# Ten output tiles in place of five, and another sequence of transfers on the sync engine's queue, in an RWKV-6 attention feeding a leaky-ReLU feed-forward layer

## The chip, the core and the metric

The kernel runs on one core of a Trainium2 chip. The core has a matrix engine (TensorE, PE in the profile, with its weight loads listed apart as PEld), three engines for elementwise work (VectorE or DVE, ScalarE or ACT, GpSimd or POOL), and a sync engine (SyncE or SP), whose only work here is to issue transfers. Sixteen DMA engines move the data between the chip's memory and the on-chip buffers. Each engine works through its own list of instructions in order, and semaphores tell one engine what another has finished. The metric is the device time of one execution in microseconds (us), as the median of several runs; less is better.

## What is computed

Four sequences of 768 positions with 8 heads of 48 numbers go through a recurrence with a state of 48x48 per head, and the result of every position, 384 numbers wide, goes through a feed-forward layer of width 2048.

```python
def _attn_ref(r, k, v, w, u):
    B, H, S, D = r.shape                      # 4, 8, 768, 48
    state = np.zeros((B, H, D, D))
    for t in range(S):
        kt, vt, rt, wt = ...
        cur = np.einsum('bhd,bhe->bhde', u[None] * kt, vt)
        y[:, :, t] = np.einsum('bhd,bhde->bhe', rt, state + cur)
        state = wt[:, :, :, None] * state + np.einsum('bhd,bhe->bhde', kt, vt)
    return y

def _moe_ref(x, w_in, w_out):                 # x: 3072 x 384
    h = x @ w_in                              # w_in: 384 x 2048
    g = np.maximum(0.01 * h, h)
    return g @ w_out                          # w_out: 2048 x 384
```

## The kernel before

**Tiling.** The 768 positions of each of the four sequences are cut into chunks of 128, which makes 24 chunks, numbered 0 to 23 in the order in which they are worked on (`seq`). Chunks 0 to 3 go two at a time through `pair`, the others through `single`. A chunk needs four loads, w, k, r and v (192 KB each, line 704 in `single`), which share one tile of the pool `in`. From them come the logarithm of the decay (ACT, line 714, tile `lw`), its running sum (PE, lines 720 and 723), its exponentials (ACT, lines 741, 746 and 750), the scaled r and k (DVE, line 403, tile `rk`), their transpose (tile `rkT`; for thirteen chunks a transposing DMA from SP, line 767, for the others PE and a copy, lines 414 to 421), the scores (PE, line 860), the masked scores (DVE, line 791, tile `m`), the bonus term of the current position (POOL, lines 433, 437 and 445, with a sum on DVE, line 441, tiles `ru`, `dg` and `vs`), the decayed state (POOL, line 778, tile `sb`), the new state (PE, line 801, and DVE, lines 814 and 816, tile `s`), and the attention's output (PE, lines 827 and 832, and DVE, line 478, tile `y`). That output is transposed into a tile of the pool `xT` (PE, ACT or DVE, lines 464 to 471; for six chunks a transposing DMA from SP, line 845).

**The layer behind it.** Fourteen blocks of one or two chunks follow (`blocks`). A block's first product reads its `xT` tile and the first weights (PE, line 1026); ACT applies the leaky ReLU (line 1041) into a tile of the pool `g`. The second product is plain for the first seven blocks (PE, line 1056; copied out on lines 1067 and 1069; stored on line 1073). For the last seven blocks `seven` does it with seven half-size products instead of eight (PE, line 956), with sums of `g` on DVE beforehand (line 937) and differences of the weights prepared once (line 906); the results are combined on ACT and DVE (lines 970, 972 and 977) in tiles of the pool `o` and stored on line 1009. Each chunk ends in a store of 192 KB from a tile of `o`; one of the last goes in two halves, so that there are 25 stores.

**What sets the order.** Nothing is reordered by a scheduler. Each piece of work is a step of a `Plan`; the table `ORDER` lists the 1124 steps by number, and `FORCE` names the engine where a step has a choice. `Plan.order` walks through `ORDER`, hands each step that opens a tile the tile of its pool that the planner thinks free first, and the steps are then written out in that order. So every engine's list is the part of `ORDER` that falls to it. The planner's times (`LOAD`, `STORE`, `TRK` and so on) choose only which tile of a pool is taken. Waits are put in by the framework: a transfer into a tile waits for the last reader of what was there, a store waits for the engine that filled the tile.

**SP's queue.** All transfers but one tiny one stand in one list on SP: 142 of them, which are loads, weights, transposes and stores. SP issues them strictly in that order. A transfer whose wait isn't over holds up all that stand behind it. It also waits, before each, for the transfer eight places earlier to have landed, as there are eight completion semaphores in turn.

```python
    make("s", 6, [128, NP, 2, D], F32)
    make("xT", 6, [128, KT, max(blocks) * L], BF16)
    make("o", 5, [128, DM], F32)
```

## Time and profile before

| | |
|---|---|
| median of 3 runs | 178.51 us (178.13 to 179.82) |
| the profiled execution: its own time | 179.84 us |
| the profiled execution: span from first to last instruction | 178.1 us |
| granted TensorE clock | 1.000 of full speed |
| bytes moved | 33.89 MB on SP's queue; 25.17 MB read, 4.72 MB written |

The profile is one execution. The profile's page gives each engine's busy time, then the span in forty slices with one digit of busy share for each, then the DMA queues, the chain of work that ended last, and the costliest groups of instructions. Beside the page the trace can be asked for the instructions of an engine in order of time, for busy times by stretch, and for who waited for whom. In the rows in order of time the columns are start and duration in us, engine, line, operation, tile written <- tiles read, shape, how many alike stand in the row, and in brackets the engine's idle time ahead of it and what ended that. SPq is SP's sequencer, whose rows last from the start of an issue until the next can go.

### The profile page before, as it was taken

The page shows a single profiled execution, that of the slowest core. Times are in us where ns is not written, and L with a number is a line of the kernel's source. Part 1 is how long each engine was busy: PE and PEld are TensorE (multiplying, and loading weights), DVE is VectorE, ACT ScalarE, POOL GpSimd, SP SyncE. Part 2 cuts the span into 40 slices and gives each one's busy share as a digit, 9 for nine tenths or more (in the row PEclk, how much of TensorE's full clock was granted, in tenths as well). Part 3 has the DMA queues.
Part 4 walks back from the last instruction along what each step waited for, and adds up shares of the span by engine and source line. Part 5 has one row for each costly group of instructions (what it writes and reads, how often), then busy time and mean ns, then how long its engine had stood idle before and what let it go on. Part 6 is the DMA issues. An engine that isn't in the chain of part 4 may idle for free. (4 is left out here: it accounts for less than half of the span.)

```text
span 178.1 us, 5529 instructions
## 1 busy us (share of the span) xinstructions
PE 169.0 (95%) x2155; PEld 139.5 (78%) x2158; DVE 142.6 (80%) x300; ACT 113.1 (64%) x262; POOL 106.1 (60%) x143
## 2 busy tenths in 40 slices
PE   6899999996999999999999999999999999999992
PEld 2555788754778877777779899799898888899992
DVE  7698735275699889879879999989999889966862
ACT  5787769814777793796369964676966671248500
POOL 5999846369759668869778384291572872700000
PEclk9999999999999999999999999999999999999999
DMA  5999998999999899899899999896999995533014
GB/s 139 261 272 342 350 298 167 358 227 211 195 190 201 154 191 229 149 199 199 169 212 171 204 192 278 161 205 136 201 205 176 204 156 109 177 90 103 32 37 145
DMA packets 115885, 34.25 MB, mean 192 GB/s; under 512 B 108305, under 2 KB 115090, under 8 KB 115858
## 3 DMA queue, kind: packets, MB, share of 16 engines
q1 hardware_dynamic: 115856, 33.89, 88.9%
q8 instruction: 17, 0.28, 0.7%
q14 instruction: 10, 0.08, 0.2%
q10 hardware_dynamic: 2, 0.00, 0.0%
HBM read 25.17 MB, written 4.72 MB: 168 GB/s over the span
## 5 line engine op out<-in xcount | busy, mean ns | idle before, releaser
L1026 PE MATMUL ps<-xT,w_in_b 128*128 128x256 bf16 (+1 forms) x672 | 71.3, 257 | 0.1
L1041 ACT ACTIVATE g<-ps 128x512 bf16<-128x512 f32 x96 | 54.5, 599 | 18.6 <-PE ps L1026 16.8
L1026 PEld LDWEIGHTS <-w_in_b 128*128 128x128 bf16 x672 | 56.8, 98 | 7.4 <-ACT w_in_b L340 0.6
L433 POOL TENSOR_TENSOR ru<-in,ub 128x384 f32<-128x384 f32 x24 | 23.9, 999 | 13.1 <-DVE dg L441 6.6
L1056 PE MATMUL ps<-w_out_b,g 128*128 128x384 bf16 x160 | 31.4, 326 | 0.0
L403 DVE TENSOR_TENSOR rk<-in,ps 128x384 bf16<-128x384 f32 x48 | 25.0, 548 | 6.0 <-ACT ps L750 2.2
L437 POOL TENSOR_TENSOR ru<-ru,in 128x384 f32<-128x384 f32 x24 | 23.8, 1000 | 5.0 <-DMA in<-in_r_dram 4.3
L791 DVE TENSOR_TENSOR m<-ps,maskb 128x512 bf16<-128x512 f32 x40 | 25.3, 683 | 0.6 <-PE ps L860 0.6
L445 POOL TENSOR_TENSOR vs<-in,dg 128x384 f32<-128x384 f32 x20 | 16.9, 844 | 11.3 <-DVE dg L441 5.1
L778 POOL TENSOR_TENSOR sb<-s,a 128x384 bf16<-128x384 f32 x18 | 14.8, 828 | 10.6 <-ACT g L1041 4.6
L1056 PEld LDWEIGHTS <-g 128*128 128x128 bf16 x160 | 14.1, 97 | 7.0 <-issue 0.2
L956 PEld LDWEIGHTS <-g 128*128 128x128 bf16 x224 | 18.4, 98 | 0.3
L441 DVE TENSOR_REDUCE dg<-ru 128x8 f32<-128x384 f32 x24 | 13.0, 547 | 5.0 <-POOL ru L437 4.8
L453 POOL CAST vb<-in 128x384 bf16<-128x384 f32 x24 | 13.2, 554 | 4.6 <-DMA in<-in_v_dram 4.0
L972 ACT COPY o<-ps 128x192 f32<-128x192 f32 x17 | 5.4, 317 | 16.0 <-PE ps L956 13.9
L714 ACT ACTIVATE lw<-in 128x384 bf16<-128x384 f32 x20 | 10.0, 520 | 7.0 <-DMA in<-in_w_dram 7.0
L977 DVE TENSOR_TENSOR o<-ps,o 128x192 f32<-128x192 f32 x35 | 11.6, 352 | 3.5 <-DMA out_dram<-o 1.3
L956 PEld LDWEIGHTS <-in 128*128 128x128 bf16 x168 | 13.6, 98 | 0.8 <-DVE in L937 0.5
L478 DVE TENSOR_TENSOR y<-ps,vs 128x384 bf16<-128x384 f32 x20 | 10.8, 552 | 2.2 <-PE ps L832 1.5
L750 ACT ACTIVATE ps<-ci 128x384 f32<-128x384 f32 x20 | 9.8, 491 | 3.8 <-DVE ci L732 3.1
L732 DVE TENSOR_TENSOR ci<-ps,lw 128x384 f32<-128x384 f32 x20 | 10.9, 551 | 1.0 <-PE ps L720 0.6
L956 PE MATMUL ps<-in,in 128*128 128x192 bf16 x112 | 11.4, 247 | 0.3 <-DVE in L937 0.3
(105 smaller groups left out, 255.2 us busy)
## 6 DMA issues: line engine op xcount, KB each, us to landing
out_dram<-o SPq DMA_DIRECT2D x23, 192.0 KB, 3.3
in<-in_w_dram SPq DMA_DIRECT2D x20, 192.0 KB, 4.7
in<-in_k_dram SPq DMA_DIRECT2D x20, 192.0 KB, 4.3
in<-in_r_dram SPq DMA_DIRECT2D x20, 192.0 KB, 4.6
in<-in_v_dram SPq DMA_DIRECT2D x20, 192.0 KB, 4.2
in<-in_moe_w_out_dram SPq DMA_DIRECT2D x4, 768.0 KB, 6.8
in<-in_moe_w_in_dram SPq DMA_DIRECT2D x2, 768.0 KB, 9.8
in<-in_moe_w_in_dram SPq DMA_DIRECT2D x4, 384.0 KB, 8.2
```

The lines of the kernel that those rows point to most:

```text
L403: (nc.gpsimd if e == "POOL" else nc.vector).tensor_tensor(out=o, in0=x, in1=i, op=ALU.mult)
L433: lambda e: nc.gpsimd.tensor_tensor(out=ru.t[:], in0=kv(), in1=ubv, op=ALU.mult),
L437: lambda e: nc.gpsimd.tensor_tensor(out=ru.t[:], in0=ru.t[:], in1=rv(), op=ALU.mult),
L441: lambda e: nc.vector.tensor_reduce(out=dg.t[:], in_=ru.t[:], axis=AX.X, op=ALU.add),
L445: lambda e: nc.gpsimd.tensor_tensor(out=vs.t[:], in0=vv(), in1=dg.t[:].unsqueeze(2).to_broadcast([128, H, D]), op=ALU.mult),
L453: {"POOL": 0.56}, lambda e: nc.gpsimd.tensor_copy(out=vb.t[:], in_=vv()),
L778: lambda e: nc.gpsimd.tensor_tensor(out=sb.t[:].rearrange("p g a d -> p (g a) d"), in0=s_in.t[:].rearrange("p g a d -> p (g a) d"), in1=a_ ...
L791: lambda e, par=par: nc.vector.tensor_tensor(out=m.t[:, par, :, :], in0=sc[par].t[:].rearrange("p (g t) -> p g t", g=NP), in1=maskb[:].uns ...
L956: nc.tensor.matmul(o(), lhsT=x()[:, i, :], rhs=y()[:, i, :], start=fresh, stop=(stop and i == ii[-1]), skip_group_check=True)
L1026: nc.tensor.matmul(hp.t[:, a * N : (a + 1) * N], lhsT=w_in_b[:, t, (j + a) * 128 : (j + a + 1) * 128], rhs=xb.t[:, t, 0:N], start=(a == 0 ...
L1041: lambda e, hp=hp, g=g, j=j, J=J, N=N: nc.scalar.activation(out=g.t[:, j : j + J, 0:N], in_=hp.t[:, 0 : J * N].rearrange("p (a n) -> p a n ...
L1056: nc.tensor.matmul(op.t[:, 0:DM], lhsT=g.t[:, j, off : off + 128], rhs=w_out_b[:, j, :], start=(j == 0), stop=(j == NJ - 1))
```

## The change

Three pools change their size: `o` from five tiles to ten, `xT` from six to three, `s` from six to five. In `ORDER`, the numbers of SP's steps are put into other places from about the 200th entry on. `FORCE`, the planner's times and all other code stay.

```diff
-    736, 770, 756, 139, 141, 140, 737, 176, 184, 186, 187, 148, 150, 164, 170, 171, 168, 169, 175, 185, 190, 191, 192,
+    736, 770, 756, 139, 141, 140, 737, 176, 148, 184, 186, 175, 187, 150, 164, 170, 171, 168, 169, 185, 190, 191, 192,
...
-    make("s", 6, [128, NP, 2, D], F32)
+    make("s", 5, [128, NP, 2, D], F32)
...
-    make("xT", 6, [128, KT, max(blocks) * L], BF16)
-    make("o", 5, [128, DM], F32)
+    make("xT", 3, [128, KT, max(blocks) * L], BF16)
+    make("o", 10, [128, DM], F32)
```

On PE, DVE, ACT and POOL the instructions stand in the same order as before; only the numbers of the tiles that they use differ in places. On SP the first 34 transfers are the same, and from the 35th on the sequence differs. Of the 25 stores, 13 stand among the first 124 transfers before and 9 in the changed kernel. The three places below are all on SP. A name such as `in8_82` is the ninth tile of the pool `in`, and the same chunk's loads can have another tile in the two kernels.

The first place is the 35th to the 45th transfer. Before, it reads as follows; `in7`, `in8`, `in10` and `in0` hold chunks 8, 9, 11 and 10, and `in2` and `in6` hold chunks 6 and 7.

```order
L1073 DMA out_0_dram<-o3_149 128x384
L704 DMA in2_76<-in_v_dram 128x8x48
L704 DMA in6_80<-in_v_dram 128x8x48
L704 DMA in7_81<-in_k_dram 128x8x48
L704 DMA in8_82<-in_w_dram 128x8x48
L704 DMA in10_84<-in_w_dram 128x8x48
L704 DMA in7_81<-in_r_dram 128x8x48
L704 DMA in8_82<-in_k_dram 128x8x48
L704 DMA in8_82<-in_r_dram 128x8x48
L704 DMA in7_81<-in_v_dram 128x8x48
L704 DMA in0_74<-in_w_dram 128x8x48
```

In the changed kernel the same stretch is this; here `in10` holds chunk 10 and `in0` chunk 11.

```order
L704 DMA in2_76<-in_v_dram 128x8x48
L704 DMA in8_82<-in_w_dram 128x8x48
L704 DMA in6_80<-in_v_dram 128x8x48
L704 DMA in7_81<-in_k_dram 128x8x48
L704 DMA in7_81<-in_r_dram 128x8x48
L704 DMA in8_82<-in_k_dram 128x8x48
L704 DMA in8_82<-in_r_dram 128x8x48
L704 DMA in10_84<-in_w_dram 128x8x48
L1073 DMA out_0_dram<-o2_144 128x384
L704 DMA in7_81<-in_v_dram 128x8x48
L704 DMA in0_74<-in_w_dram 128x8x48
```

The store has gone from the front, chunk 9's r is two places earlier (43rd to 41st), chunk 10's w three places earlier (45th to 42nd), and chunk 11's w five places later (40th to 45th).

The second place is around the transposes of chunks 16 and 17 (`rk2` and `rk1`), the 84th to the 93rd transfer before.

```order
L704 DMA in7_81<-in_v_dram 128x8x48
L704 DMA in0_74<-in_k_dram 128x8x48
L704 DMA in0_74<-in_w_dram 128x8x48
L1073 DMA out_0_dram<-o2_148 128x384
L704 DMA in10_84<-in_k_dram 128x8x48
L1073 DMA out_0_dram<-o1_147 128x384
L1073 DMA out_0_dram<-o3_149 128x384
L1073 DMA out_0_dram<-o0_146 128x384
L767 DMA_TRANSPOSE rkT1_98<-rk2_94 128x8x128
L767 DMA_TRANSPOSE rkT0_97<-rk1_93 128x8x128
```

In the changed kernel they are the 89th and the 90th transfer, and the rows from the 83rd are these.

```order
L704 DMA in7_81<-in_v_dram 128x8x48
L1073 DMA out_0_dram<-o9_151 128x384
L704 DMA in8_82<-in_k_dram 128x8x48
L704 DMA in0_74<-in_k_dram 128x8x48
L1073 DMA out_0_dram<-o6_148 128x384
L704 DMA in0_74<-in_w_dram 128x8x48
L767 DMA_TRANSPOSE rkT0_97<-rk2_94 128x8x128
L767 DMA_TRANSPOSE rkT1_98<-rk1_93 128x8x128
```

Two stores stand among the six transfers ahead of the two transposes where four stood among the eight, and none stands directly ahead.

The third place is the loads of chunks 20 to 23. Before, the 109th to the 119th transfer are these, with chunk 20 in `in6`, 21 in `in4`, 22 in `in2` and 23 in `in7`.

```order
L1009 DMA out_0_dram<-o4_150 128x384
L704 DMA in4_78<-in_k_dram 128x8x48
L704 DMA in7_81<-in_w_dram 128x8x48
L704 DMA in2_76<-in_k_dram 128x8x48
L704 DMA in4_78<-in_r_dram 128x8x48
L704 DMA in2_76<-in_w_dram 128x8x48
L704 DMA in2_76<-in_r_dram 128x8x48
L704 DMA in6_80<-in_v_dram 128x8x48
L767 DMA_TRANSPOSE rkT1_98<-rk1_93 128x8x128
L767 DMA_TRANSPOSE rkT0_97<-rk4_96 128x8x128
L704 DMA in4_78<-in_v_dram 128x8x48
```

In the changed kernel the same work is the 106th to the 115th, with chunk 20 in `in4`, 21 in `in6` and 22 in `in7`.

```order
L1073 DMA out_0_dram<-o0_142 128x384
L704 DMA in6_80<-in_k_dram 128x8x48
L704 DMA in4_78<-in_v_dram 128x8x48
L704 DMA in7_81<-in_w_dram 128x8x48
L704 DMA in6_80<-in_r_dram 128x8x48
L704 DMA in7_81<-in_k_dram 128x8x48
L767 DMA_TRANSPOSE rkT0_97<-rk1_93 128x8x128
L704 DMA in7_81<-in_r_dram 128x8x48
L767 DMA_TRANSPOSE rkT1_98<-rk4_96 128x8x128
L704 DMA in6_80<-in_v_dram 128x8x48
```

Chunk 22's w is five places earlier (114th to 109th) and chunk 21's v four (119th to 115th), with eight stores ahead of them in place of twelve; chunk 23's r, a little further on, goes from the 122nd place to the 118th. The stores that have left these stretches stand behind the last load, among the 125th to the 137th transfer.

78 rows, old and new, of the table ORDER are left out of this document.

## The prediction

> **What bounds the kernel now.** I read the page first, then busy times by stretch, then PE's instructions in order of time, then what stands before each of PE's stops.
>
> ```profile
> PE 169.0 (95%) x2155; PEld 139.5 (78%) x2158; DVE 142.6 (80%) x300; ACT 113.1 (64%) x262; POOL 106.1 (60%) x143
> ...
> DMA  5999998999999899899899999896999995533014
> ...
> q1 hardware_dynamic: 115856, 33.89, 88.9%
> ```
>
> ```profile
> 50.00:75.00 25.00, 24.74 (x319) 19.38 (x318) 23.10 (x44) 17.63 (x41) 18.29 (x22) 1.00 0.98 185
> ...
> 100.00:125.00 25.00, 24.72 (x334) 22.68 (x332) 23.24 (x47) 16.62 (x44) 11.97 (x15) 1.00 0.94 196
> 125.00:150.00 25.00, 24.27 (x324) 21.70 (x323) 23.80 (x48) 16.22 (x43) 15.48 (x19) 1.00 0.95 180
> 150.00:170.00 20.00, 20.00 (x231) 18.61 (x230) 15.56 (x37) 9.86 (x19) 3.90 (x5) 1.00 0.32 95
> ```
>
> PE (the third number of a stretch) is close to full from 50 us on. The 16 DMA engines are as full: their share, the last but one number, is 0.94 to 0.98 up to 150 us, and the page's digits are 8s and 9s till then. So there are two full resources, PE and the one queue that SP feeds. What the change can touch is the places where PE stops because that queue is late. These are PE's rows around its stops.
>
> ```profile
> 41.51 0.32 PE L720 MATMUL ps<-lw,trev 128*128 128x384 bf16 x1 [1.85 <-ACT lw L714]
> ...
> 67.02 0.83 PE L1026 MATMUL ps<-xT,w_in_b 128*128 128x256 bf16 x6
> 68.11 0.40 PE L860 MATMUL ps<-rkT 48*128 48x128 bf16 x8 [0.26 <-DVE rkT L419]
> ...
> 113.89 0.40 PE L860 MATMUL ps<-rkT 48*128 48x128 bf16 x8
> 114.56 0.40 PE L860 MATMUL ps<-rkT 48*128 48x128 bf16 x8 [0.28 <-DVE dg L441]
> 114.89 0.83 PE L956 MATMUL ps<-in,in 128*128 128x192 bf16 x8
> ...
> 137.04 0.24 PE L723 MATMUL ps<-ones,lw 128*128 128x1 bf16 x4
> 137.36 0.33 PE L801 MATMUL ps<-vb,rk 128*128 128x96 bf16 x4
> ...
> 144.81 0.41 PE L956 MATMUL ps<-in,g 128*128 128x192 bf16 x3
> 145.59 0.33 PE L827 MATMUL ps<-sb,rkT 128*128 128x96 bf16 x4 [0.36 <-POOL sb L778]
> ...
> 148.83 0.74 PE L956 MATMUL ps<-in,g 128*128 128x192 bf16 x7
> 149.85 0.83 PE L956 MATMUL ps<-in,in 128*128 128x192 bf16 x8 [0.29 <-DVE in L937]
> ```
>
> The stop at 41.51 (1.85 us) is the largest, but its load stands among SP's first 34 transfers, which stay; it gets nothing. Five stops are left. How much a stop costs is the start after it less the start that PE's pace would have given. The pace comes from the chain of work that ended last (start, length, what):
>
> ```profile
> 115.73 1.31 PE ps L1026 x12
> ...
> 126.87 0.08 PE ps L723 x4
> ...
> 131.40 4.88 DMA in<-in_w_dram
> ...
> 157.79 5.91 PE ps L1026 x54
> ...
> 166.98 7.93 PE ps L956 x96
> ```
>
> One matmul of L1026 takes 1.31/12 = 5.91/54 = 0.109 us, one of L956 7.93/96 = 0.083, four of L723 0.08; eight of L860 take 114.89 - 114.56 = 0.33. The five stops then cost 68.11 - 67.02 - 6x0.109 = 0.43; 114.56 - 113.89 - 0.33 = 0.34; 137.36 - 137.04 - 0.08 = 0.24; 145.59 - 144.81 - 3x0.083 = 0.53; 149.85 - 148.83 - 7x0.083 = 0.44. Together 1.98 us. The idle times in the brackets alone are 0.26 + 0.28 + 0.36 + 0.29 = 1.19.
>
> That the pace is the same 0.109 in two stretches is also the answer to a question of the Trainium skill: its page Perfetto Trace Analysis, section Identifying the Most-Contended Engine, says that matmul busy time is a poor measure of the distance to the limit and that weight-load time should be used. By that, PE at 78% (139.5 of 178.1) would have up to 38.6 us in hand, an estimate from that page; the equal pace in these rows leaves 1.98 behind the 34th transfer, and I go by the rows.
>
> **What ended the stops.** One row for each, of the engine that waited for the queue:
>
> ```profile
> 62.05 0.55 DVE L403 TENSOR_TENSOR rk<-in,ps 128x384 bf16<-128x384 f32 x1 [0.53 <-DMA in<-in_r_dram]
> ...
> 114.56 0.23 PEld L860 LDWEIGHTS <-rkT 48*128 48x128 bf16 x8 [0.45 <-DMA rkT<-rk]
> ...
> 136.30 0.52 ACT L714 ACTIVATE lw<-in 128x384 bf16<-128x384 f32 x1 [1.36 <-DMA in<-in_w_dram]
> ...
> 143.47 0.83 POOL L445 TENSOR_TENSOR vs<-in,dg 128x384 f32<-128x384 f32 x1 [1.31 <-DVE ci L732]
> ```
>
> These are chunk 9's r, the transposes of chunk 17, chunk 22's w and chunk 21's v. In the last row the profile names a sum on DVE, which L445 does not read; it reads v, and v's issue and usual time to landing point to about 142.7 (138.47 + 4.2) or later:
>
> ```profile
> 108.57 0.54 DVE L403 TENSOR_TENSOR rk<-in,ps 128x384 bf16<-128x384 f32 x1
> ...
> 107.63 2.85 SPq L767 DMA_TRANSPOSE rkT<-rk  x2
> ...
> 138.47 0.57 SPq L704 DMA_DIRECT2D in<-in_v_dram  x1
> ...
> in<-in_v_dram SPq DMA_DIRECT2D x20, 192.0 KB, 4.2
> ...
> rkT<-rk SPq DMA_TRANSPOSE x13, 4.0
> ...
> 105.50 2.02 SPq L1073 DMA_DIRECT2D out_dram<-o  x3
> ```
>
> The fifth stop (149.85) is the fourth one's echo: DVE's add for the chunk, L478, runs behind PE's 145.59, and its sums of L937 behind that.
>
> **The change, part by part.** *The sequence.* No transfer is added or dropped, so the queue has as much to do as before; what it does earlier is loads, what it does later is stores. A place in the queue is worth on average 88.9% of 178.1 us over 142 transfers = 1.1 us; a store less, 2.02/3 = 0.67 by the row at 105.50. Chunk 9's r loses one store and one load ahead of it: 1.8 us earlier, where DVE stood idle 0.53; stop 1 goes (0.43). Chunk 22's w loses four stores and a load, 3.8 us, where ACT waited 1.36; stop 3 goes (0.24). Chunk 21's v loses four stores, 2.7 us, where POOL waited 1.31. Stop 4 goes, but then DVE is next: it is busy 23.80 of 25 us there and runs the sums of stop 5 in its own order, so of 0.53 + 0.44 I take back 0.55 and keep 0.42. The transposes of chunk 17 can't be issued earlier than their `rk`, which DVE finishes at 108.57 + 0.54 = 109.1, in the middle of SP's row of the two transposes; only the queue ahead is shorter. They took from about 109.2 to 114.56, 5.4 us, against a median of 4.0. Between 0 and 0.34 I take half, 0.17. Sum: 0.43 + 0.17 + 0.24 + 0.42 = 1.26 us.
>
> *Loads that move back.* Chunk 11's w goes from the 40th to the 45th place, where chunk 10's w stood. By the next row ACT takes the logarithms of chunks 11 and 10 without a stop between, so whatever stood 45th had landed by about 63.3, and chunk 11's can begin 0.4 us later than its 62.87.
>
> ```profile
> 62.87 0.93 ACT L714 ACTIVATE lw<-in 128x384 bf16<-128x384 f32 x2
> ...
> 66.79 0.48 ACT L1069 COPY o<-ps 128x384 f32<-128x384 f32 x1 [0.20 <-PE ps L1056]
> 67.88 0.60 ACT L1041 ACTIVATE g<-ps 128x512 bf16<-128x512 f32 x1 [0.61 <-PE ps L1026]
> ```
>
> Behind it on ACT stand copies of transposes and leaky ReLUs; ACT's idle 0.20 and 0.61 take up the 0.4. Bounds: 0 and a loss of 0.4; I take 0, since idle time of twice that follows within 5 us.
>
> *Stores at the end.* The stores set back go out behind the last load, in the stretch from 150 us on, where the DMA share is 0.32. They cost nothing while they are through before the last stores, whose end is the kernel's; bounds 0 and 0.67, one store in front of the last one, and I take 0.
>
> *Ten tiles in `o`.* They let stores wait. They also end one wait for a tile, 1.28 us on DVE, but PE is full in that stretch (20.00 of 20), so it gives nothing.
>
> ```profile
> 160.71 0.36 DVE L977 TENSOR_TENSOR o<-ps,o 128x192 f32<-128x192 f32 x1 [1.28 <-DMA out_dram<-o]
> ```
>
> *Three tiles in `xT`, five in `s`.* A new writer waits for the readers three blocks back. The closest such pair in the new assignment is 11 us apart, so no wait:
>
> ```profile
> 31.30 0.83 PE L1026 MATMUL ps<-xT,w_in_b 128*128 128x128 bf16 x12
> ...
> 43.44 0.36 DVE L469 COPY xT<-ps 128x384 bf16<-128x384 bf16 x1
> ```
>
> For `s`, with five tiles for four sequences, a new state (DVE L816) overwrites one that POOL has read for a chunk further back; bounds 0 and, were a pair late, its lateness; I take 0.
>
> **Sum.** The profiled execution took 179.84 us for a span of 178.1. Less 1.26 that is 178.58, a ratio of 0.993; on the median of 178.51, which is 1.33 below the profiled execution, it is 177.3 us.
>
> **The rivals.**
> - *All stops go.* DVE follows PE without being late itself, and the 1.98 us come back: 176.5. For it: DVE's sums start right after PE's product each time. Against: DVE's 23.80 of 25.
> - *Nothing comes back.* The queue is as full as before and only four stores have left it ahead of chunk 21; transposes still wait for DVE's `rk` and hold the loads behind them; or DVE at 93 to 95% stops PE instead at the same places. Then the time is 178.5, or 178.1 with one or two stops gone. For it: the five stops end by four different engines. Against: in four of the five an engine stood idle 0.45 to 1.36 for the queue alone.
> - *PE's busy time hides waits.* Then earlier loads could give more than 1.98 us and the time would lie below 176.5. For it: L860's and other small matmuls, whose pace I took from one pair of rows. Against: the equal pace of L1026 in both stretches, and 20.00 of 20 us busy where the queue is light. The Trainium skill's page Perfetto Trace Analysis, named above, is on its side.
> - *Chunk 11's w is late, and the kernel slower.* The pattern is the stop at 41.51, where a late w cost PE 1.85. If the eleven transfers from the 35th on take longer than before, ACT stands at L714, with the copies of transposes and the leaky ReLUs queued behind it, and PE stops at its running sum. It decides from about 0.8 us of lateness on (ACT's two idle times); each us beyond costs one. With the stop of 1.85 again and the gain of 1.26 kept, 179.1; slower by over 1% needs more than 3 us beyond, or a lost gain as well.
>
> **How the numbers follow.** The forecast, a gain of 0.6 to 1.75 us (176.8 to 177.9), has 56%; all stops gone, 16%; hidden waits, 2%; nothing, 16%; slower, 10%. The likeliest is 177.3. The range reaches from 176.3 (all stops, and a little of the noise of 0.4 between the first two runs) to 178.9 (nothing comes back, or a small loss), and leaves out the larger losses and the rest, some 15%. About 1% is what a measurement of this kernel can tell from no change: faster by that is below 176.7, nearly all of "all stops go" and "hidden waits" and a little of the forecast, 20%; slower by that is above 180.3, most of the third rival, 8%; the rest, 72%, is within.
>
> **What would show it.** Right: no idle time of PE ahead of L860 near 68 and near 114, of L801 near 137 and L827 near 145; no DVE wait for chunk 9's r, no ACT wait ahead of L714 near 136; stop at 41.5 unchanged; PE's last matmul near 173.6 instead of 174.9. Stop 5 smaller but still there, ended by DVE. Wrong: an ACT wait at L714 near 63 followed by a PE stop; a stop where none stood, ended by DVE or by a transpose; or the store of the last chunk landing later than before behind its last DVE add.

## The result, and the profile after

| | before | after |
|---|---|---|
| median of 20 runs each | 180.06 us (177.98 to 181.89) | 177.69 us (176.94 to 179.40) |
| profiled execution, its own time | 179.84 us | 177.21 us |
| its span | 178.1 us | 175.4 us |
| PE's last matmul ends | 174.90 us | 172.43 us |

The ratio after to before is 0.9931, with a 95% interval of 0.9903 to 0.9959: a gain of 0.7%, small but clear of no change. The ratio counts only the runs in the faster of two states, while the medians in the table count all 20 and would give 0.987. In two later groups of runs, 12 of the kernel after beside 35 of the kernel before on one chip each, it is 0.997 (0.9941 to 0.9998; medians 177.54 and 178.28) and 0.9948 (0.9924 to 0.9973; 177.42 and 178.41). The kernel after has nearly the same median all three times. The kernel before was 1.7 us longer in the first group than in the others.

From the page of the kernel after: busy time of the engines, the digits of DMA, and the queue that SP feeds.

```profile
PE 168.8 (96%) x2158; PEld 139.4 (79%) x2158; DVE 142.8 (81%) x300; ACT 113.5 (65%) x262; POOL 107.0 (61%) x143
...
DMA  5999998999999899999999988897999996652404
...
q1 hardware_dynamic: 115856, 33.89, 94.0%
```

Busy time by stretch of the kernel after (us of the stretch, then PE, PEld, DVE, ACT, POOL, granted clock, DMA share, GB/s):

```profile
50.00:75.00 25.00, 25.00 (x317) 19.68 (x315) 23.45 (x44) 18.14 (x42) 19.25 (x22) 1.00 1.05 185
...
100.00:125.00 25.00, 25.00 (x337) 22.95 (x335) 24.14 (x49) 17.01 (x45) 12.07 (x16) 1.00 0.90 171
125.00:150.00 25.00, 25.00 (x342) 22.94 (x340) 24.75 (x49) 15.39 (x41) 16.27 (x20) 1.00 0.98 172
150.00:170.00 20.00, 20.00 (x232) 18.67 (x230) 13.93 (x37) 9.87 (x19) 3.35 (x5) 1.00 0.41 132
```

PE now fills every stretch from 50 us on, where it had 24.74, 24.72 and 24.27 of 25. DVE does the same work in the shorter time, 24.75 of 25 us in the busiest stretch. PE's instructions in the kernel after, at the places where it stopped before (start, length, engine, line, operation, tile written <- tiles read, shape, count, and in brackets the idle time ahead):

```profile
41.07 0.32 PE L720 MATMUL ps<-lw,trev 128*128 128x384 bf16 x1 [1.52 <-ACT lw L714]
...
67.34 0.40 PE L860 MATMUL ps<-rkT 48*128 48x128 bf16 x8
...
112.90 0.77 PE L860 MATMUL ps<-rkT 48*128 48x128 bf16 x16
...
135.84 0.33 PE L801 MATMUL ps<-vb,rk 128*128 128x96 bf16 x4
...
143.57 0.33 PE L827 MATMUL ps<-sb,rkT 128*128 128x96 bf16 x4
...
148.71 0.82 PE L956 MATMUL ps<-in,in 128*128 128x192 bf16 x8
```

Only the stop for chunk 6's w, near 41, is left. The other five have no bracket.

To see where the time went I use one measure from here on, **PE's lag**: the start of a matmul in a profile, less the start of the same matmul in this profile of the kernel after. The list of PE's instructions is the same in all, so the lag grows exactly where a kernel loses time against the kernel after. At the kernel after's 44, 60, 100, 120, 130, 136, 144, 150 and 170 us the profile of before lags by 0.44, 0.43, 0.99, 1.30, 1.29, 1.56, 2.01, 2.47 and 2.47 us. So 0.44 us stem from the first 44 us, where both kernels have the same sequence, and 2.03 from the rest: the 1.98 us of the five stops, within the error of such sums. The forecast took 1.26 of them.

### The profile page after: what moved, and what is told of

It is laid out like the page before. It is cut to its first block, busy times and chain, and to the rows that moved or that the text cites. A ratio compares the mean times of both kernels' runs of the same rounds, so it can differ in the third digit from the quotient of the medians.

```text
span 175.4 us, 5523 instructions
## 1 busy us (share of the span) xinstructions
PE 168.8 (96%) x2158; PEld 139.4 (79%) x2158; DVE 142.8 (81%) x300; ACT 113.5 (65%) x262; POOL 107.0 (61%) x143
## 4 chain that ended last, share of the span: by engine, by line
PE 75%; SPq 14%; DMA 7%; issue 1%; POOL 1%; ACT 0%; DVE 0%; POOLq 0%
PE ps L1026 30%; PE ps L956 19%; PE ps L1056 12%; SPq L490 5%; DMA in<-in_k_dram 4%; SPq L314 4%; SPq L704 3%; PE ps L860 3%; DMA in<-in_w_dram 3%; PE ps L832 2%; SPq L319 2%; PE ps L827 2%; PE ps L720 2%; PE ps L801 1%; PE ps L414 1%; PE ps L464 1%
## 5 line engine op out<-in xcount | busy, mean ns | idle before, releaser
L433 POOL TENSOR_TENSOR ru<-in,ub 128x384 f32<-128x384 f32 x24 | 24.4, 1021 | 9.6 <-issue 5.7
L778 POOL TENSOR_TENSOR sb<-s,a 128x384 bf16<-128x384 f32 x18 | 15.3, 856 | 13.6 <-DVE s L816 6.3
L445 POOL TENSOR_TENSOR vs<-in,dg 128x384 f32<-128x384 f32 x20 | 17.2, 859 | 5.7 <-DVE dg L441 3.7
L453 POOL CAST vb<-in 128x384 bf16<-128x384 f32 x24 | 13.0, 545 | 5.7 <-DMA in<-in_v_dram 5.7
L714 ACT ACTIVATE lw<-in 128x384 bf16<-128x384 f32 x20 | 10.0, 521 | 3.9 <-DMA in<-in_w_dram 3.9
L478 DVE TENSOR_TENSOR y<-ps,vs 128x384 bf16<-128x384 f32 x20 | 10.8, 552 | 2.0 <-PE ps L832 2.0
L956 PE MATMUL ps<-in,g 128*128 128x192 bf16 x112 | 11.5, 246 | 0.0
```

The lines of the kernel that those rows point to most:

```text
L433: lambda e: nc.gpsimd.tensor_tensor(out=ru.t[:], in0=kv(), in1=ubv, op=ALU.mult),
L445: lambda e: nc.gpsimd.tensor_tensor(out=vs.t[:], in0=vv(), in1=dg.t[:].unsqueeze(2).to_broadcast([128, H, D]), op=ALU.mult),
L453: {"POOL": 0.56}, lambda e: nc.gpsimd.tensor_copy(out=vb.t[:], in_=vv()),
L778: lambda e: nc.gpsimd.tensor_tensor(out=sb.t[:].rearrange("p g a d -> p (g a) d"), in0=s_in.t[:].rearrange("p g a d -> p (g a) d"), in1=a_ ...
L956: nc.tensor.matmul(o(), lhsT=x()[:, i, :], rhs=y()[:, i, :], start=fresh, stop=(stop and i == ii[-1]), skip_group_check=True)
```

## Experiments: are the five stops there every time?

`pools_only` is the kernel before with the new numbers of tiles and the old sequence.

```diff
-    make("s", 6, [128, NP, 2, D], F32)
+    make("s", 5, [128, NP, 2, D], F32)
...
-    make("xT", 6, [128, KT, max(blocks) * L], BF16)
-    make("o", 5, [128, DM], F32)
+    make("xT", 3, [128, KT, max(blocks) * L], BF16)
+    make("o", 10, [128, DM], F32)
```

> Kernel before with the tile counts of the kernel after (ten o, three xT, five s) and the old sequence of SyncE. Theory A (the sequence carries the gain, the tiles only permit it): the five PE stops of before (68.1, 114.6, 137.4, 145.6, 149.9 us, 1.98 us in sum) are all still there, ratio to before 1.000, within 0.997 to 1.003. Theory B (the tiles themselves free DVE and ACT from waits): DVE's wait of 1.28 us on an o tile near 160.7 goes and with it part of the stops, ratio near 0.993. Fewer xT and s tiles: neither theory expects a new PE wait for them.

Ratio 0.9982 (0.9944 to 1.0021). Neither theory held in full: the tiles alone bring nothing that can be measured, but the five stops were not there either. That asked for a second and a third profile of the kernel before, unchanged, and for more of the kernel after.

> The kernel before, unchanged, for a second profile of it. The kernel with the old sequence and ten o tiles showed none of the five stops at their size, only 0.10 us at 131.7 and 0.08 at 136.4. Theory A (the stops of 0.26 to 0.36 us in the first profile of before are of that one execution, whose loads landed late: chunk 9's r at 61.95, 1.7 us later behind its neighbour than the 1.05 us that a load takes): the second profile has at most two PE stops behind 60 us, under 0.3 us in sum, and a span near 176.5. Theory B (the stops belong to the old sequence with five o tiles, and it was the tiles that took them away): four or five stops stand again with 0.8 to 1.2 us in sum, span near 178.

> The kernel before, unchanged, for a third profile. Theory A (of the five stops only the one for chunk 22's w is a usual one): PE's lag grows by 0.3 to 0.9 us from 130 to 136 us, by landing less lag less 134.72, and by under 0.2 us in all between 50 and 130 us. Theory B (the stops near 68 and 146 come often): a growth of 0.3 us or more at either.

> The kernel after, unchanged, beside the kernel before on one chip, and a second profile of it. Theory A (its loads land early enough that late ones cost nothing): no PE stop over 0.1 us behind 60 us again; ratio to before 0.993 to 0.996 (on the chip of the second group of runs, whose median of before is 178.3). Theory B (the gain was that of the chip or the executions compared): ratio 0.998 to 1.002.

> The kernel after, unchanged, a third time, to stand beside the others of this group: ratio 0.994 to 0.998, no growth of the lag.

`before_again` against the kernel before: 1.002 (0.9986 to 1.0054), as it should be; `before_third` was one run, 178.64 us. The ratio of `after_again`, 0.997, lies between those of its two theories; its profile, without a stop behind 60 us, is that of theory A. `after_third` came out as expected. The lags, worked out from the starts in each trace:

| kernel after's time, us | 44 | 60 | 100 | 120 | 130 | 136 | 144 | 150 | 170 | grown from 50 to 170 |
|---|---|---|---|---|---|---|---|---|---|---|
| before, first profile | 0.44 | 0.43 | 0.99 | 1.30 | 1.29 | 1.56 | 2.01 | 2.47 | 2.47 | 2.03 |
| before_again | 0.37 | 0.37 | 0.37 | 0.41 | 0.40 | 1.26 | 1.19 | 1.19 | 1.19 | 0.82 |
| before_third | 0.38 | 0.38 | 0.39 | 0.45 | 0.48 | 0.56 | 0.48 | 0.91 | 1.07 | 0.69 |
| pools_only | 0.15 | 0.15 | 0.16 | 0.01 | 0.04 | 0.65 | 0.57 | 0.72 | 0.72 | 0.57 |
| after_again | 0.34 | 0.34 | 0.34 | 0.20 | 0.18 | 0.18 | 0.22 | 0.22 | 0.22 | -0.12 |
| after_third | 2.45 | 2.45 | 2.61 | 2.55 | 2.53 | 2.53 | 2.46 | 2.46 | 2.46 | 0.01 |

In three more profiles the old sequence loses 0.57 to 0.82 us behind 50 us, not 2.03, and not at fixed places: 0.86, 0.08 and 0.61 between 130 and 136, and 0.43 in one of the three at 147. (So `before_third` went against its theory A, which expected 0.3 us or more by 136, and nearer to B, with its loss at 147.) The stop at 68 (0.43 us in the forecast) belongs to the first profile alone; chunk 9's r, at 61.95 there, landed at 59.99, 59.81 and 59.77 in the others. The loss near 114, 0.31 there, is 0.06 at most in the others. The kernel after's three profiles differ by less than 0.2 us behind 50 us. (The lag of 2.45 that its third has from the first 44 us is the matter of the last section.)

The three waits of PE in `before_third` that are longest (us in total, times, longest):

```profile
PE ps L720 <- ACT lw L714: 1.5, 1, 1.5
...
PE ps L860 <- DMA rkT<-rk: 0.4, 1, 0.4
```

and of `after_again`:

```profile
PE ps L720 <- DVE dg L441: 1.8, 1, 1.8
PE ps L1095 <- DVE zeros L257: 1.3, 1, 1.3
```

In the first list stands the stop at 147, 0.4 us for the transposes of chunk 23, that the profile of the prediction hadn't shown. In the second nothing stands but chunk 6's w (the profile names a DVE sum that ended last) and the start of the kernel.

**A deadline for chunk 22's w.** Most of the loss ahead of 136 follows one load. ACT's logarithm L714 starts as the load lands, and PE's L801 for that chunk comes later by what L714 is late. From `before_again`, then `pools_only`, then the kernel after, the logarithm and the matmul:

```profile
136.00 0.52 ACT L714 ACTIVATE lw<-in 128x384 bf16<-128x384 f32 x1 [1.66 <-DMA in<-in_w_dram]
```

```profile
137.05 0.33 PE L801 MATMUL ps<-vb,rk 128*128 128x96 bf16 x4
```

```profile
135.38 0.52 ACT L714 ACTIVATE lw<-in 128x384 bf16<-128x384 f32 x1 [1.33 <-DMA in<-in_w_dram]
```

```profile
136.45 0.33 PE L801 MATMUL ps<-vb,rk 128*128 128x96 bf16 x4
```

```profile
133.37 0.54 ACT L714 ACTIVATE lw<-in 128x384 bf16<-128x384 f32 x1
```

Take the lag just ahead, at 132 us (0.59 and 0.32), off L714's start to put it on the kernel after's clock: 136.00 - 0.59 = 135.41 and 135.38 - 0.32 = 135.06. L801 came 137.05 - 135.84 - 0.59 = 0.62 and 0.29 us late. The difference is 134.79 and 134.77: that is the deadline. The lag drops out of it, so it says this much: where L801 waits for this load, it starts 1.06 us after L714 does, and 135.84 - 1.06 = 134.78. That holds within 0.02 us in the seven profiles that lost time here, among them before's first (135.01, loss 0.23) and `before_third` (134.81, loss 0.03), and in the others, where L714 started earlier, L801 lost nothing. In the kernel after L714 starts at 133.37, 1.4 us ahead of it.

The rest of the loss between 130 and 136, 0.19 us in `before_again` and 0.28 in `pools_only`, belongs to a second load, chunk 19's v, which is the 108th transfer in the old sequence and the 103rd in the new one. POOL's copy of v (L453) waited for it, DVE's sum y (L478) for POOL, and the weight loads of PE's transposes of y (L464) for DVE. From `pools_only`, two instructions and a row of its waits from 130 to 133 us:

```profile
128.86 0.50 POOL L453 CAST vb<-in 128x384 bf16<-128x384 f32 x1 [0.71 <-DMA in<-in_v_dram]
```

```profile
131.15 0.56 DVE L478 TENSOR_TENSOR y<-ps,vs 128x384 bf16<-128x384 f32 x1 [0.19 <-POOL vs L445]
```

```profile
PEld L464 <- DVE y L478: 0.3, 1, 0.3
```

In the kernel after this v landed at 126.89 and nothing waited for it.

## Experiments: which part of the change?

The kernels of this section have the tiles of the kernel after. `loads_new` has its order of loads, with the stores put back. In these diffs only SP's numbers in `ORDER` stand, at the first place, against the kernel after; 760 and 746 are stores, 297 is chunk 9's r.

```diff
-    217, 206, 295, 226, 264, 265, 296, 297, 327, 746, 266, 350, 407, 328, 298,
+    217, 206, 295, 760, 226, 264, 265, 296, 297, 327, 266, 350, 407, 328, 746, 298,
...
```

> Kernel after with its new order of loads among themselves, but with the stores of results put back to the places they had before. By what stands ahead in SyncE's sequence (load 1.08 us, store 0.67, transposes 1.25), against before: chunk 9's r 1.1 us earlier, chunk 22's w 1.1 earlier, the transposes of chunk 17 1.1 later, chunk 21's v and chunk 23's r unchanged. Theory A (what stands ahead in the sequence decides each stop): the stops near 68.1 and 137.4 go, those at 114.6, 145.6 and 149.9 stay, that at 114.6 grows; ratio 0.996 to 1.001. Theory B (the order of the loads is the change, the stores cost nothing because the queue takes them beside loads): all five stops go, ratio near 0.993.

`stores_new` is the reverse: old order of loads, new places of stores.

```diff
-    217, 760, 206, 226, 264, 295, 350, 265, 296, 297, 266, 327, 746, 409,
+    217, 206, 226, 264, 295, 350, 265, 746, 296, 297, 266, 327, 409,
...
```

> Kernel before's order of loads among themselves, with the stores put where the kernel after has them, and its ten o tiles. By what stands ahead, against before: chunk 9's r unchanged, the transposes of chunk 17 2.6 us earlier, chunk 22's w 2.7, chunk 21's v 2.7, chunk 23's r 2.6 earlier. Theory A (what stands ahead decides; the deferred stores carry most of the gain): the stop at 68.1 stays with 0.3 to 0.4 us, the other four go, 1.55 us in sum, ratio 0.989 to 0.994. Theory B (the loads' own order is needed): three or more of the four stay, ratio over 0.996.

`front_new` has the first 51 transfers of the kernel after and then the old order (the stores 760 and 788 and the load 409 follow as 52nd to 54th); `tail_new` has the first 105 of the kernel before and then the new order:

```diff
     573, 617,
-    618, 562, 934, 637, 693, 668, 638, 667, 669, 619, 630, 650, 639, 694,
+    562, 618, 693, 637, 619, 667, 638, 668, 630, 669, 650, 639, 694, 970,
...
```

> Kernel after's sequence for the first 51 transfers, the kernel before's order for the rest: the first place of the change alone. Chunk 9's r lands near 58.3, 1.5 us ahead of where two of three profiles of the old sequence have it (59.8 and 60.0), and these two show no stop for it. Theory A (the stop at 68.1 in the first profile of before was that of one execution): the lag grows by 0.5 to 0.9 us from 130 to 136 us as with the old sequence, and the ratio is 0.9985 to 1.001. Theory B (the first place brings the 0.43 us that the first profile shows): ratio 0.9975 or lower.

> Kernel before's sequence for the first 105 transfers, the kernel after's order for the rest, ten o tiles: the third place of the change alone. Chunk 22's w 1.8 us earlier, chunk 21's v and chunk 23's r 0.7 and 0.6. Theory A (that place carries the gain of a usual execution): no growth of PE's lag from 130 to 150 us over 0.2 us, ratio 0.995 to 0.998, as the kernel after on this chip (0.997). Theory B (the first two places carry half or more): ratio over 0.9985.

| | ratio to before (95%) | lag at 44 | 50 | 110 | 130 | 136 | 150 | 170 |
|---|---|---|---|---|---|---|---|---|
| loads_new | 0.9967 (0.9942 to 0.9992) | -0.02 | -0.02 | -0.02 | 0.55 | 0.54 | 0.47 | 0.47 |
| stores_new | 0.9998 (0.9967 to 1.0030) | 0.63 | 0.63 | 0.63 | 0.72 | 1.06 | 1.11 | 1.11 |
| front_new | 1.0024 (0.9991 to 1.0057) | 0.49 | 0.49 | 0.49 | 0.54 | 0.63 | 0.86 | 0.86 |
| tail_new | 0.9969 (0.9946 to 0.9993) | -0.59 | 0.62 | 0.62 | 0.47 | 0.65 | 0.58 | 0.58 |

The expectation for `stores_new` failed: with the stores out of the way but the loads in their old order, chunk 22's w still missed its deadline (0.34 us at 136), and no gain is measured. Counting places had promised that it would land 2.7 us earlier; it landed at 135.77, between the 135.27 and 136.28 of the old sequence. For `loads_new` the count erred the other way: 1.1 us promised, and it landed at 132.65, with the time 0.33% shorter although two stops of 0.3 us came near 114 and 123. So for chunk 22's w it is the order of the loads that counts. For the time as a whole the ratios point to the loads as well, 0.9967 against 0.9998, but the two intervals overlap, and the lags do not tell the two parts apart: from 50 to 170 us they grow by 0.49 and 0.48. What the lags do tell is the place, with one profile each. `tail_new` has the ratio that the kernel after had in the group before (0.997) and on balance loses nothing from 50 us on (an early landing of chunk 6's w put PE 0.59 ahead at 44, and other early loads took that back by 50). `front_new` gains nothing in time, though its lag grew by only 0.09 from 130 to 136, where 0.5 to 0.9 was expected.

## Experiments: one load at a time

`w22_swap` is the kernel before, five `o` tiles, with two numbers exchanged, chunk 22's w (667) and k (668). It ran twice.

```diff
-    647, 637, 651, 693, 668, 633, 1021, 967, 649, 1009, 638, 646, 648, 667, 671, 958, 1008, 961, 989, 673, 674, 965,
+    647, 637, 651, 693, 667, 633, 1021, 967, 649, 1009, 638, 646, 648, 668, 671, 958, 1008, 961, 989, 673, 674, 965,
```

> Kernel before, five o tiles, with one exchange: the loads of chunk 22's w (114th of SyncE's transfers) and of chunk 22's k (112th) trade places. Over seven profiles, PE's lag at 136 us behind the kernel after grows by 0.86, 0.61, 0.34 and 0.27 us where chunk 22's w landed at 135.57, 135.32, 135.05 and 135.00 on the kernel after's scale (landing less lag), and not where it landed ahead of 133: a deadline of 134.72 that explains each within 0.02. Theory A (in a usual execution this one load is most of what the change brings): it lands two places, about 2.1 us, earlier, near 133.7, ahead of its deadline; no growth of the lag from 130 to 136 over 0.1 us; from 44 to 170 the lag grows by under 0.35 us in place of 0.57 to 0.82; ratio 0.996 to 0.998. Theory B (the gain needs the whole new sequence): growth of 0.5 us or more from 44 to 170, ratio 1.000 within 0.002.

> The kernel before with the loads of chunk 22's w and k exchanged, once more, for a profile at the full granted clock; its first one had the clock at 0.5 of full speed for 3.4 us and loads late by 2 us, and its ratio was 1.001. Theory A (the lateness passes on: PE reaches its next needs earlier and finds them late): the stop at 136 us is gone, and from 138 to 150 us the lag grows by 0.4 us or more; ratio 0.999 to 1.001. Theory B (a gain that the first group of runs did not resolve): lag growth from 44 to 170 us under 0.3 us, ratio 0.996 to 0.998.

Ratios 1.0012 (0.9984 to 1.0040) and 1.0028 (0.9998 to 1.0057): no gain, as theory B of the first expectation has it, though in both profiles the lag stays put from 132 to 140 (2.73 in the one, 2.74 in the other; 2.3 and 2.5 of it are from the first 44 us, for the reason of the last section, and 0.24 and 0.13 were lost at 131.5 to chunk 19's v). A loss came ten us later. From the second profile, POOL's product with chunk 21's v and PE's matmul that needs it:

```profile
144.97 0.83 POOL L445 TENSOR_TENSOR vs<-in,dg 128x384 f32<-128x384 f32 x1 [1.20 <-DMA in<-in_v_dram]
```

```profile
147.08 0.33 PE L827 MATMUL ps<-sb,rkT 128*128 128x96 bf16 x4 [0.68 <-POOL sb L778]
```

This is the fourth stop of the prediction, with the profile now naming the load of v itself. It has a deadline too: L445's start less the lag ahead of it is 142.30 here, 142.55 in the first profile of the swap and 141.98 in that of before, and the lag grew by 0.83, 1.08 and 0.52 us: 141.47 each time within 0.01. So PE was no longer held up for w and met v late, as theory A of the second expectation has it. But PE lost 1.08 and 0.83 us there, more than the 0.6 that it had gained over `before_again`: v landed 5.2 and 5.0 us after its issue, where `before_again` has 3.3 and before's first profile 4.9. Why, no run shows. The second run was meant to bring a profile at the full clock and did not; both have the half clock near 43. So that the lateness passes from one load to the next is seen twice here and not shown to follow from the exchange. The kernel after has moved both loads.

`w22_back` is the kernel after with that one load put back by three transfers, behind 638, 668 and the transposes 630.

```diff
-    637, 619, 667, 638, 668, 630, 669, 650,
+    637, 619, 638, 668, 630, 667, 669, 650,
```

> Kernel after with one load put back: chunk 22's w from the 109th to the 112th place, behind the loads of chunk 21's r and chunk 22's k and the transposes of chunk 21. By 1.08 us a load and 1.25 the transposes it lands 3.4 us later, at 135.7 to 136.4. Theory A (deadline of 134.72): PE's lag behind the kernel after grows from 130 to 136 us by landing less deadline, 1.0 to 1.7 us, the wait is PE's L720 for ACT's L714, and the ratio to before is 1.002 to 1.006. Theory B (other work moves into the gap, the deadline is not one): growth under 0.5 us, ratio under 1.000.

Ratio 1.0126 (1.0089 to 1.0162): one transfer moved by three places costs more than the whole change brings. (Three of the six runs had a mean clock of 0.99 and took 181.07 to 181.45 us, the others 179.3 to 179.8.) The load came later than I had counted, and L714 and PE's stop behind it read:

```profile
137.10 0.52 ACT L714 ACTIVATE lw<-in 128x384 bf16<-128x384 f32 x1 [3.52 <-DMA in<-in_w_dram]
```

```profile
137.68 0.32 PE L720 MATMUL ps<-lw,trev 128*128 128x384 bf16 x1 [1.83 <-ACT lw L714]
...
138.16 0.37 PE L801 MATMUL ps<-vb,rk 128*128 128x96 bf16 x4
```

L714 stands at 137.10 - 0.11 = 136.99, by the deadline of 134.78 a loss of 2.21; L801 is 138.16 - 135.84 - 0.11 = 2.21 late. The other 1.6 us of the lag of 3.9 come right behind, from the granted clock (last section).

`k20_only` is the kernel before with chunk 20's k (617) moved from the 106th to the 94th transfer, ahead of four transposes; SP's numbers:

```diff
-    518, 538, 559, 527, 581,
+    518, 538, 617, 559, 527, 581,
...
-    593, 573, 617, 618, 562, 934,
+    593, 573, 618, 562, 934,
```

> Kernel before, five o tiles, with one number moved: the load of chunk 20's k from the 106th to the 94th of SyncE's transfers, ahead of the four transposes whose issue keeps SyncE from 117.7 to 123.9 us while the queue runs partly dry (DMA share 0.66 of 16 engines from 120 to 125 us, 0.83 to 1.16 around it). Chunk 22's w stays the 114th. Theory A (a load moved into that stretch is gone from the full queue behind it): every load behind 124 us lands about 1.1 us earlier, chunk 22's w at 134.3 to 134.9; PE's lag behind the kernel after grows by under 0.3 us from 130 to 136 us (0.61 and 0.86 with the old sequence), ratio 0.996 to 0.999. Rival B: the transposes of chunk 17 or the output transposes near 122 us come later by the load now ahead of them, and a stop of 0.2 to 0.3 us near 115 or 123 takes the gain: ratio 0.999 to 1.001.

Ratio 0.9974 (0.9938 to 1.0009), which does not tell the two apart. The profile does: rival B. A new stop stands where the output transposes now come late,

```profile
123.36 1.81 PE L1026 MATMUL ps<-xT,w_in_b 128*128 128x256 bf16 x15 [0.79 <-DMA xT<-y]
```

the lag grows by 1.01 us from 120 to 130, and chunk 22's w landed at 135.30, hardly earlier. That PE then met it in time (135.32 - 0.74 = 134.58, ahead of 134.78) is only because PE itself was late.

## Experiments: is DVE the next bound?

The forecast held back 0.55 us because DVE would be next. These two kernels add reductions on DVE to the kernel after, in the stretch of the fourth and fifth stop.

```diff
+        spare = pool.tile([128, 1], F32, name="spare")
         for i in order:
+            if i in (649, 648):
+                nc.vector.tensor_reduce(out=spare[:], in_=zeros[:, 0:384], axis=AX.X, op=ALU.add)
```

This is `dve_one`, with two of them; `dve_half` has one, ahead of step 649 alone.

> Kernel after with one extra VectorE reduction of 128x384 (about 0.5 us, result not used) put ahead of the L403 that starts at 133.88 us. Theory A (VectorE is the next bound where the stops of 145.6 and 149.9 were, it keeps up with nothing in hand): a PE stop of 0.4 to 0.55 us appears within 10 us of it, and the time is 0.3 to 0.55 us longer than that of the kernel after: ratio to before about 0.9955 where the kernel after has 0.993. Theory B (VectorE, busy or not, has half a microsecond in hand there): no PE stop, ratio 0.993.

> Kernel after with two extra VectorE reductions of 128x384 (0.535 us each as the run with one has it, results not used), ahead of the two L403 that start at 133.88 and 134.35 us. The run with one such reduction showed no PE stop over 0.1 us. Theory A (VectorE has nothing in hand there, and PE loses what is added, if not in one stop then in many under 0.06 us): PE's time from the end of the chunk 6 stop to its last matmul is 0.9 to 1.1 us over that of the kernel after (131.36 us in its profile; 131.72 with one reduction), ratio to before 0.005 to 0.006 above that of the kernel after. Theory B (half to one us in hand): under 0.4 us over it, ratio within 0.002 of the kernel after.

Busy time from 135 to 140 us of the kernel after, of `dve_half` and of `dve_one` (PE first, DVE third):

```profile
135.00:140.00 5.00, 5.00 (x69) 4.44 (x68) 5.00 (x12) 3.96 (x12) 4.68 (x6) 1.00 0.92 180
```

```profile
135.00:140.00 5.00, 4.92 (x58) 4.29 (x57) 5.00 (x12) 3.63 (x11) 4.61 (x5) 1.00 1.10 193
```

```profile
135.00:140.00 5.00, 4.44 (x51) 3.96 (x50) 5.00 (x12) 2.84 (x9) 3.27 (x5) 1.00 0.83 162
```

PE's lag grew from 130 to 140 us by 0.41 for the one reduction of 0.535 us and by 0.99 for two of 0.54. By the lag that is theory A: DVE has next to nothing in hand there. The times do not settle it. For two reductions the median is 178.12, where the kernel after had 177.54 in the same group, but the ratios, 0.998 (0.9953 to 1.0007) and 0.997, differ by 0.001, which is theory B's figure. For one (177.21, ratio 0.9945 from 0.9915 to 0.9976) there is no kernel after in the group. The measure that the second expectation named, from the stop for chunk 6's w to PE's last matmul, gives 2.2 us more than the kernel after, above both theories: in that profile PE was 1.04 us ahead at 44 and had given back 0.88 of it by 60, long before the reductions.

## Experiments: the stop that is left

The stop near 41 is for chunk 6's w, the 25th transfer. `w6_one` exchanges it with the 24th, chunk 5's k; `w6_late` with the 26th, a half of the output weights. Both start from the kernel after.

```diff
-    176, 148, 175, 203, 142, 204,
+    176, 148, 203, 175, 142, 204,
```

> Kernel after with the load of chunk 6's w one place earlier in SyncE's sequence (24th, ahead of chunk 5's k). Theory A (the stop of 1.5 us at 39.6 is the landing of that load alone): it lands 1.0 us earlier, the stop shrinks to 0.3 to 0.6 us, and the time falls by 0.5 to 1.0 us: ratio to before 0.003 to 0.006 below that of the kernel after. Rival B (the queue is full until 47 us, so chunk 5's k or chunk 6's k and r become the late ones): the stop shrinks but another of 0.3 us or more opens between 37 and 50 us, and the ratio is that of the kernel after within 0.002.

> The kernel after with the load of chunk 6's w ahead of that of chunk 5's k, once more beside the kernel after. In its first profile the stop at 39.6 us was gone and one of 1.75 us stood at 42.4, for chunk 5's k; its 12 runs had none of the lower mean clock of 0.99. Theory A (the queue, not the order of the two, sets this stop): median within 0.2 us of the kernel after. Theory B (the later stop is less often long enough to cost the clock): no run at a mean clock of 0.99 again, median 0.3 us or more below the kernel after.

Ratios 0.9948 (0.9926 to 0.9969; median 177.43) and 0.9951 (0.9927 to 0.9975; 177.58), where the kernel after stood at 0.997 and 0.9948 (177.54 and 177.42): the same time. The profile says why. PE runs 1.8 us ahead of the kernel after at 42 us and stops there instead, since chunk 5's k is now late:

```profile
44.12 2.06 PE L1026 MATMUL ps<-xT,w_in_b 128*128 128x128 bf16 x34 [1.75 <-DVE xT L469]
```

So this stop is the queue's, and the order of these two only moves it. One sign of theory B did come: none of the 24 runs of this kernel had a mean clock of 0.99, where 4 of the 24 of the kernel after in the same groups did (179.4 to 179.82 us). The lower median that theory B asks for did not, so that stays open. I found no version that is measurably faster than the kernel after.

## Why the prediction was wrong, and what in it was right

The forecast ratio was 0.993 and the measured one is 0.9931; the forecast time of 177.3 stands beside 177.69. That agreement is luck. The sum behind the forecast, a gain of 1.26 us, is neither the 2.03 us that the two compared profiles differ by behind 50 us nor the 0.57 to 0.82 us that the old sequence loses in the other profiles, and the later groups of runs have 0.997 and 0.9948. The mechanism was right: loads that land earlier end stops of PE. Two steps failed, the bound under which a move counts as no change, and the five stops of one execution taken as the usual loss, with 0.55 of them wrongly held back.

- *"About 1% is what a measurement of this kernel can tell from no change."* This step failed. No row stood behind the bound, and it was too coarse: with 20 runs of each kernel the interval is 0.6% wide, and 0.7% is a clear gain. The 72% for a move within 1% went by that bound: the measured move lies in that band, and still it is a gain, not the absence of one.
- *"The five stops then cost … Together 1.98 us."* The sum was right for that execution and wrong as a property of the kernel. The second step that failed is taking one profile, 1.33 us longer than the median of its own three runs, as the usual case. By three more profiles the old sequence loses 0.57 to 0.82 us there. The first stop, 0.43 of the sum of 1.26, appears in no other profile.
- *Stop 4 and 5: "then DVE is next … of 0.53 + 0.44 I take back 0.55."* This is the term of the sum that was mis-sized: between the two profiles nothing of the 0.55 was lost, and stop 5, foretold as smaller but still there, is gone. The reason behind it was right, for half a microsecond more on DVE does cost PE 0.4; but DVE just keeps up, and a resource that just keeps up costs nothing. The rival *all stops go* described the profile.
- *Stop 2: "between 0 and 0.34 I take half."* The lag from 110 to 120 tells: two profiles with the transposes landing at 111.75 and 111.95 (`pools_only`, `after_again`) run 0.14 to 0.15 us ahead of the kernel after, where they landed at 113.22, and before's first lost 0.31 to it. So about 0.15 is left of that stop in the kernel after's profile, and nothing in its second.
- *Stop 3.* Gone as foretold. Its 0.24 was the smallest of the five and it is the one that comes back, with up to 0.6.
- *The place in the queue at 1.1 us, a store 0.67.* Landing times, transfer by transfer from the trace, are 4.0 us earlier for chunk 22's w (forecast 3.8) and 3.2 for chunk 21's v (2.7), but 3.6 for chunk 9's r (1.8). `stores_new`, `loads_new` and `w22_back`, counted in the same way, were off by 0.6 to 3 us. I put this down to stretches in which SP waits ahead of transposes and the queue has no next transfer at hand (the DMA share falls to 0.66 from 120 to 125 us in `before_again`); no run isolates it.
- *Chunk 11's w moved back: 0.* Right. It landed at 62.15, ACT takes both logarithms without a stop, and no PE stop follows:

```profile
62.44 0.93 ACT L714 ACTIVATE lw<-in 128x384 bf16<-128x384 f32 x2
```

- *"Stop at 41.5 unchanged."* Its cause is, its length isn't: 1.52, 1.78 and 2.03 us in the kernel after's three profiles, as that load's landing moves from 40.47 to 41.25 with nothing changed ahead of it.
- *PE's last matmul "near 173.6".* It was 172.43: 0.72 from the stops that I kept, 0.44 from the first 44 us, which no part of the change touches.
- *Stores at the end: 0.* From PE's last matmul to the end of the span there are 3.2 us before and 3.0 after, and 3.2 to 3.4 in `before_again`, `before_third` and `front_new` against 3.0 to 3.1 in `after_again`, `tail_new` and `w6_one`; but `k20_only`, with the old stores, has 3.0 too. This quarter of a microsecond I have not traced.

Open is also why the kernel before took 180.06 us in the first group and 178.3 in the others. That the new sequence bears a late queue better would fit, as in the kernel after the work on chunk 22's w starts 1.4 us and that on chunk 21's v 1.0 us (L445 at 140.44) ahead of its deadline, but it was not tested.

## What to carry to other kernels

Before costing a change by the stops in a profile, compare the profiled execution's own time with the median, and where it is longer, look at a second profile: small stops of a full queue move about. Turn a stop into a deadline (start of the first instruction on the load, less PE's lag just ahead, less the loss): from when a load lands it gives what PE loses, in other executions and other orders, to hundredths. When a load will land it doesn't say, and counting places in the queue didn't either. And look at all loads that run close to their deadline: with chunk 22's w alone moved, the time stayed the same here, and in both profiles the next one was late.

## What was not expected of the hardware

PE's granted clock can fall to half after a stop of about 2 us. Stretches of `after_third`, whose stop was 2.03 us, and of `front_new`, whose stop was 1.93 us (PE first, the granted clock before the DMA share):

```profile
41.85 0.32 PE L720 MATMUL ps<-lw,trev 128*128 128x384 bf16 x1 [2.03 <-ACT lw L714]
```

```profile
42.00:44.00 2.00, 2.00 (x12) 1.02 (x11) 0.56 (x1) 1.03 (x4) 1.24 (x2) 0.55 0.77 111
44.00:46.00 2.00, 2.00 (x14) 1.37 (x13) 0.80 (x3) 1.45 (x3) 1.42 (x3) 0.60 0.98 190
46.00:48.00 2.00, 2.00 (x36) 1.94 (x35) 1.46 (x3) 0.94 (x2) 1.51 (x2) 1.00 1.29 218
```

```profile
41.56 0.32 PE L720 MATMUL ps<-lw,trev 128*128 128x384 bf16 x1 [1.93 <-DVE dg L441]
```

```profile
42.00:44.00 2.00, 2.00 (x19) 1.35 (x18) 1.07 (x3) 1.32 (x5) 1.53 (x2) 1.00 0.72 115
44.00:46.00 2.00, 2.00 (x35) 1.94 (x34) 1.03 (x3) 1.90 (x4) 1.32 (x3) 1.00 1.07 207
```

PE counts as busy throughout in both, but does 26 matmuls in four us at the lower clock and 54 at the full one. The clock was low for (2 x 0.45 + 2 x 0.40) / 0.5 = 3.4 us and back by 46 us. `w22_swap` and its repeat, with stops of 1.99 and 2.12, show the same; the stops of 1.78 to 1.93 in four other profiles don't; and the stop of 1.83 in `w22_back`, at another place, does. The lag then grows by 1.7 us in each, which goes with runs of the kernel before at a mean clock of 0.99 taking about 180.2 us in the later groups and most others about 178.3. The Trainium skill's page TensorE: Matmul & The Clock Gate, section Part 1: The HAM clock gate, has the half clock, and some 3.4 us of work until the full one is granted again, and these rows agree; but it puts the idle time needed at a window of about 3.4 us, and here 2.0 sufficed. The measurement decides. I made the stop longer to see whether it is the cause:

```diff
-    148, 175, 203, 142, 204,
+    148, 175, 142, 203, 204,
```

> The kernel after with chunk 6's w one place later, behind a half of the output weights (26th in place of 25th): by the 2.27 us that such a load takes it lands near 42.8, and the stop that was 1.52 and 1.78 us long is 3.7 to 4.1. Three profiles with this stop at 1.99, 2.03 and 2.12 us have the granted clock at 0.5 for some 3.4 us behind it, four with 1.78 to 1.93 us do not. Theory A (PE standing still for about 2 us costs the clock): every run has a mean clock near 0.99, the profile shows the 0.5 behind the stop, and the time is 2.3 us for the landing and 1.5 us for the clock over the kernel after, 181.0 to 181.6: ratio 1.014 to 1.020. Theory B (the drop and the long stop are both signs of a disturbed execution): the clock stays at 1.0 in most runs, and the time is 179.6 to 180.0, ratio 1.006 to 1.011.

Ratio 1.017 (1.0127 to 1.0213), median 181.48. The stop was 3.62 us, the clock stood at 0.50 from 41.9 to 48.7 us in the profile, so it fell 1.1 us before the stop was over and stayed low for 6.8 us, and three of the four runs had a mean clock of 0.991, 0.990 and 0.981 (181.46, 181.50 and 182.36 us). The fourth had 0.999 and 180.20 us. So a long stop mostly costs the clock, but not every time.

Where the bound lies can be read from the traces. In all 20 profiles the granted clock changes only at ticks 3.413 us apart, counted from its first rise to full: in `after_third` it rises at 4.65, falls at 42.20, which is 11 ticks later, and rises at 45.61. What tells the cases apart is how long PE stands idle between two ticks, which is the length of such a stretch less PE's busy time. Stretches from tick to tick of `after_third`, then two of `front_new`, then two of `w22_back`:

```profile
38.78:42.20 3.42, 1.39 (x23) 0.90 (x20) 2.38 (x5) 0.52 (x1) 2.31 (x3) 1.00 1.13 299
```

```profile
38.03:41.44 3.41, 1.60 (x23) 1.08 (x21) 2.25 (x5) 0.45 (x1) 2.86 (x4) 1.00 1.10 291
41.44:44.86 3.42, 3.30 (x37) 2.45 (x37) 1.82 (x5) 2.14 (x7) 2.39 (x3) 1.00 0.90 154
```

```profile
39.34:42.75 3.41, 1.57 (x14) 0.92 (x13) 2.07 (x5) 0.86 (x3) 1.68 (x3) 1.00 1.12 249
134.91:138.32 3.41, 1.49 (x19) 1.13 (x17) 2.34 (x6) 1.22 (x4) 1.65 (x2) 1.00 0.94 179
```

The clock fell at the end of the first and of the last, with 2.03 and 1.92 us idle, and not at the end of the other three, with 1.81, 0.12 and 1.84: a tick cut `front_new`'s stop of 1.93 in two. Over all 20 profiles the clock fell behind every one of the 13 such stretches with 1.92 us or more (eight of them at the kernel's end, where PE has run out of work) and behind none of the 978 with 1.84 or less. This is read from the profiles; no run moved a stop against the ticks. A stop of 3.6 us that a tick cuts into two halves would leave the clock up, as in the fourth run of `w6_late`, but that run has no profile. A stop of 1.5 to 2.1 us, as this kernel has near 41, stands right at the bound: 0.3 us of a load's landing, or the place of a tick, then decide over 1.7 us more.
